# One fused attention, expert and Fourier kernel: value products moved next to the scores, correction products in 128 rows, a relu moved ahead of the folds

## The chip, the cores and the metric

The kernel runs on one core of a Trainium2 chip. The metric is the device time of one execution in microseconds, from the profiler's clock on the chip. Three runs of the kernel before gave 562.93, 563.63 and 563.84 us (median 563.63). TensorE multiplies into PSUM, VectorE and ScalarE read PSUM and work on SBUF, POOL (GpSimd) works on SBUF and issues the indirect transfers, and SP issues most of the other transfers. Each engine runs its own list of instructions in order and waits on semaphores for the others.

## The reference

Three stages in float32. `B,H,S,D` is 2, 8, 768, 64, and the width after the heads are joined is 512.

```python
# attention: a window of 16 around each position, and 24 block maxima of k
k_sum = k.reshape(B, H, nb, block, D).max(axis=3); v_sum = v.reshape(B, H, nb, block, D).mean(axis=3)
scores_l = scale * q @ k.T                      # masked to abs(i-j) < window
scores_s = scale * q @ k_sum.T + np.log(block)
a = softmax(concat([scores_l, scores_s]))       # divided by its sum + 1e-9
x = a @ concat([v, v_sum])
# experts: one of 8 for each token, in order of position
e = argmax(logits) if s == 0 or local_gate < 0.5 else the expert of the token before
out[b, s] = p[e] * (np.maximum(x[b, s] @ w1[e], 0.0) @ w2[e])
# Fourier mix and dense layer
u = x + np.real(fft(fft(x, axis=1), axis=2))
un = (u - mean(u)) / np.sqrt(var(u) + 1e-06)
return u + np.maximum(un @ w_ch1, 0.0) @ w_ch2
```

## The kernel before, in words

**Attention** (`attention`, lines 45 to 257) runs 24 steps t of 128 queries and four heads: 2 batches, 2 groups of heads (a unit u is a batch with a group), 6 chunks. A step is spread over six steps of the loop. `S1(t)` makes the scores on TensorE: two products of the mask `maskb` (69 rows) and sixteen passes of small products of 64 rows and 64 columns (L124), into `sc`. `D1(t)` takes their maximum on VectorE, `A1(t)` the exponentials `a` on ScalarE. Two steps later `S3` transposes `a` into `pa` (L144), `A3` copies it to `att` on ScalarE. One step later again `S4` multiplies `att` with the window of v, `vw`, into `po` (L153): eight products, each into 64 of the 128 partitions, the output's last column being the sum of the weights. `D4` divides on VectorE. `S5` transposes the result into `px` (L169), `A5` copies it to `xT`, and `S6` multiplies it with the gate (L178, into the bank `big`): the logits. So step t on TensorE holds S1 of t, S6 of t-5, S3 of t-2, S4 of t-3 and S5 of t-4, in the order in which the code of the loop calls them. `pa`, `po` and `px` have one buffer each. In steps 8, 13 and 18 `prep_v2` transposes the block means of v (`pv`, L106); ScalarE scales them into `vss` (L108) and copies them into `vw` (L111), ahead of that step's copy of `att`.

**Routing** is a Python generator (`Routing.early`) whose instructions the attention loop takes a few at a time from step 16 on: `ex.d()` gives VectorE's next one, `ex.p()` TensorE's next one, if it is that engine's turn. The logits' first half is copied to `lg` on ScalarE at step 16 (L277). The chain goes by way of the products of `val` (L305, step 17), `lr` (L308, step 18), `cnb` (L329, step 19) and `rinc` (L321, step 20). At L336 it writes the number of the first expert to `ei`; SP reads that and loads the expert's weights (`wr`, 4 of 1 MB, L502). Later it writes the first tokens' indices; POOL gathers them (`xg`, L475). TensorE transposes them (`pt`, L482), and the first expert's products follow (L527).

**Experts** (`moe`): seven slots of 256 tokens, four steps each (L520, L554). The last slot is number 6. `act` applies the relu to `ph` on ScalarE (`hh`, L544) and leaves the residue on VectorE (`hl`, L545); both are operands of `L2` (L554). `out` scales (`y`, L559) and scatters by POOL (L561).

**Fourier mix** (`fft_ffn`, a generator too, whose pieces `next(fft)` puts among slot 6's last products). Sums, differences and halves of rows (`foldE`, `foldP`, `foldO`, `foldQ`, L771 to L787) prepare the operands on VectorE with copies on ScalarE; then products with the tables (L796), corrections of few rows (L811 with 33, L827 with 34 rows), splits into two parts for precision (L767). Batch 0 goes first; `xload(1)` (L722) loads batch 1 once slot 6 is scattered. Then the normalised rows go through the dense layer (L907, L918), where TensorE works without a pause to the end.

The order on each engine is that of the code: nothing moves it afterwards (`manual_schedule`).

Of the kernel before, what the change touches and what calls it, by code (L numbers as in the profile page):

```python
# [15 lines left out]
def keep_warm(nc,I,ps,n):  # L16

    for _ in range(n): nc.tensor.matmul(ps,lhsT=I['busy'][:,0:128],rhs=I['busy'][:,0:ps.shape[-1]],start=True,stop=True)
# [30 lines left out]
def attention(tc,ctx,cp,I,ident,x_dram,plg,late,hook,ex):  # L49
# [3 lines left out]
    with tc.tile_pool(name="at2",bufs=2) as p2, tc.tile_pool(name="at1",bufs=1) as p1, \  # L53
# [94 lines left out]
        def S4(t):  # L148
            u,c=divmod(t,6)
            po=ppo_.tile([128,4,65],F32,name=f"po{t}",tag="po")  # L150
            for g in range(4):
                for jj in range(2):
                    T.matmul(po[64*jj:64*jj+64,g],lhsT=att[t%2][0:121,g,64*jj:64*jj+64],rhs=vw[u][0:121,2*c+jj,g],start=True,stop=True)  # L153
            st['po',t]=po
        def D4(t):
            u,c=divmod(t,6); b,hg=U[u]
# [33 lines left out]
        def at_(f,t):  # L190
            if 0<=t<NT: f(t)
        for t in range(NT+5):
            u,c=divmod(t,6)
            for w in LOADS.get(t,()): load(*w)
            if t<NT:
                at_(S1,t); at_(S6,t-5)
                if t>16: ex.p()
                at_(S3,t-2)
                if t in (8,13,18): prep_v2(u if t<17 else 3)
                if t==3: keep_warm(nc,I,I['idle'],N_B)  # L200
                at_(S4,t-3)
            else: at_(S3,t-2); at_(S4,t-3); at_(S5,t-4); at_(S6,t-5)
            todo=PREP.get(t,())
            at_(D1,t)
            if t<NT:
                if t==16: hook(-1,None)
                if t>16: ex.p()
                at_(S5,t-4)
            at_(D4,t-3)
            for w in todo:  # L210
                if w[0]=='k': prep_k(*w[1:])
            at_(A3,t-2)
            if t==2: keep_warm(nc,I,I['idle'],N_E); prep_v2(0)
            if t==23: at_(A1,t); at_(A5,t-4)
            else: at_(A5,t-4); at_(A1,t)
            for w in todo:
                if w[0]=='k2': prep_k2(*w[1:])
                if w[0]=='v': prep_v(w[1])
            if t==0: load(1,'k'); load(1,'q')
            if t==1: late(); keep_warm(nc,I,WP,N_D); prep_v(0)  # L220
            if t==2: prep_v3(0,V.tensor_copy,2,6); [prep_v3(0,G.tensor_copy,j,j+2) for j in (6,8,10)]
            if t in (8,13,18):
                for j in range(2,12,2): prep_v3(u if t<17 else 3,G.tensor_copy,j,j+2)
            hook(t,psc_)
            if t==NT+4: sctx.close()
# [239 lines left out]
def moe(tc,ctx,fctx,I,ident,idx,sidx,pslot,ei,x_dram,x2_dram,rt,begin,w0,NST=7):  # L465
# [46 lines left out]
    def L1(s,c,fbs=(0,1)):  # L512
        _,wh,wl=Wt[s,c]; xh,xl=X[s][-2:]
        if 0 in fbs: H[s,c]=D['ph'][c%2] if s=='d' else P['ph'].tile([128,2,256],F32,name=f"ph{s}_{c}",tag="ph")
        for fb in fbs:
            n=0
            for kd in range(4):
                o=slice(kd*256+fb*128,kd*256+fb*128+128)
                for a,b in ((wh,xh),(wh,xl),(wl,xh)):
                    T.matmul(H[s,c][:,fb],lhsT=a[:,o],rhs=b[:,kd],start=n==0,stop=n==11); n+=1  # L520
# [20 lines left out]
    def act(s,c):  # L541
        ph=H[s,c]
        hh,hl=D['h'] if s=='d' else [P['p2'].tile([128,2,256],R,name=f"h{n}{s}_{c}",tag=f"h{n}",bufs=2) for n in "hl"]
        S.activation(hh,ph,AF.Relu)  # L544
        V.scalar_tensor_tensor(out=hl,in0=ph,scalar=0.0,in1=hh.bitcast(F32),op0=ALU.max,op1=ALU.subtract)  # L545
        H[s,c]=(hh,hl)
# [33 lines left out]
    for k in range(4,n-1):  # L580
# [4 lines left out]
        s,c=steps[k]  # L585
# [35 lines left out]
            fft=I['fft'](P,D['wr']+[new('up',[128,2048],F32,"wr2","wr",bufs=3)])  # L621

    s=NST-1
    next(fft); L1(s,3); next(fft); act(s,3); L2(s,2,(0,)); next(fft); L2(s,3,(0,)); out(s,tts=(0,)); next(fft); L2(s,2,(1,)); L2(s,3,(1,))
    out(s,tts=(1,)); pctx.close()
    for _ in fft: pass

# [7 lines left out]
def lay_fft():  # L635
    j=np.arange(384)[:,None]; k=np.concatenate([[384,0],np.arange(384)])[None]
    cN=np.cos(2*np.pi*((j*k)%768)/768); cN[:,1]=0
    sN=np.sin(2*np.pi*((j*np.arange(384)[None])%768)/768)
    m=np.arange(256)[:,None]; l=np.arange(258)[None]
    cD=np.cos(2*np.pi*((m*l)%512)/512); cD[:,257]=0  # L640
    sD=np.sin(2*np.pi*((m*np.arange(256)[None])%512)/512)
    out=[]
    for t,n in ((cN,3),(sN,3),(cD,2),(sD,2)):
        for a in _split(t):
            out.append(a.reshape(n,128,-1).transpose(1,0,2).reshape(128,-1))
    ft=np.ascontiguousarray(np.concatenate(out,1)).astype(np.float32)
    corr=np.where(k%2==0,0.0,-2.0); corr[0,1]=0
    alt=np.where(l%2==0,1.0,-1.0)
    rows=np.zeros((34,386+258),np.float32); rows[[0,32],:386]=corr; rows[[0,1,32,33],386:]=alt/2
    return ft,rows  # L650
FT,FROWS=lay_fft()
def lay_ffn(w1,w2):
# [40 lines left out]
class Tables:  # L693

    def __init__(self,tc,I,tp):
        nc=tc.nc
        self.ft=tp.tile([128,FT.shape[1]],R,name="ft"); self.fr=tp.tile([34,644],R,name="fr")
        self.nc=nc; self.I=I
    def load(self,i,n):

# [3 lines left out]
    def parts(self):  # L704
        off=0; tabs=[]
        for w,n in ((386,3),(386,3),(384,3),(384,3),(258,2),(258,2),(256,2),(256,2)):
            tabs.append(self.ft[:,off:off+w*n].rearrange("p (a k) -> p a k",a=n)); off+=w*n
        return tabs,self.fr[0:33,0:386],self.fr[:,386:644]

def fft_ffn(tc,ctx,fctx,tctx,cctx,plctx,I,ident,x2_dram,out,W,P,raw):  # L710

# [43 lines left out]
    if 1:  # L755
# [4 lines left out]
        xo=[unA.tile([128,512],F32,name=f"xo{i}",tag="un",bufs=4) for i in range(4)]; tmp=[xx[:,1542:1800],xo[3][:,0:258]]  # L760
        V.memset(xe[:,:,512:514],0.0)
        V.memset(eps,1e-6); S.activation(nb[:,0:1],eps,AF.Sqrt)
        rP=p1.tile([33,258],R,name="rP"); S.activation(rP,I['busy'][0:33,0:258],AF.Copy,scale=0.0)
        xr=p1.tile([1,512],F32,name="xr")
        S2={}; ST={}; nx=[0]
        def split(dst,src,eng=None):
# [30 lines left out]
        def step1_begin(b):  # L797
            pt,qt=[P['p2'].tile([128,2048],R,name=f"t{n}{b}",tag="w"+n,bufs=3) for n in "hl"]
            ST[b]=([[pt[:,772*mb+386*i:772*mb+386*i+386] for i in range(2)] for mb in range(2)],
                   [[qt[:,768*mb+384*i:768*mb+384*i+384] for i in range(2)] for mb in range(2)],  # L800
                   P['p2'].tile([128,2,256],R,name=f"FF{b}",tag="hh",bufs=2).rearrange("p a b -> p (a b)")[0:34,0:386])
            S.activation(ST[b][2],I['busy'][0:34,0:386],AF.Copy,scale=0.0)
        SP={}
        def step1P(b,a):
            if a==0: SP[b]=[ps1.tile([128,386],F32,name=f"s1_{b}_{mb}",tag="s1") for mb in range(3)]
# [51 lines left out]
            S.copy(U(b,0,1)[0:1],S2.pop(('r',b)))  # L857
            if b==0: S.copy(acc[0:1,:,1],rs[:,0:2])
        yield
        foldE(0,0,V); foldP(0,0); foldO(0,0)  # L860
        yield
        foldE(0,1,V); foldPl(0,0); foldR(0); foldP(0,1)
        yield
# [89 lines left out]
def whole(tc,I,out):  # L953
    nc=tc.nc
    with ExitStack() as ctx:
        ctx.enter_context(tc.manual_schedule())
        cp=ctx.enter_context(tc.tile_pool(name="cp",bufs=1))
        dp=ctx.enter_context(tc.tile_pool(name="dp",bufs=1,space=bass.MemoryType.DRAM))
        x_dram=dp.tile([1664,512],F32,name="x_dram"); x2_dram=dp.tile([1664,512],F32,name="x2_dram")
        ident=cp.tile([128,128],F32,name="ident"); make_identity(nc,ident)  # L960
        busy=cp.tile([128,512],BF,name="busy"); nc.gpsimd.memset(busy,1.0); I=dict(I,busy=busy)
        idx=cp.tile([128,NT2],I32,name="idx"); sidx=cp.tile([128,NT2],I32,name="sidx"); pslot=cp.tile([128,NT2],F32,name="pslot"); ei=cp.tile([1,16],I32,name="ei")
        w0=ctx.enter_context(tc.tile_pool(name="w0",bufs=1)); W={}
        rctx=ExitStack(); rc=rctx.enter_context(tc.tile_pool(name="rc",bufs=1,side="right"))
# [45 lines left out]
```

## Time and profile before

| | us |
|---|---|
| median of three runs | 563.63 |
| the profiled execution's own time | 563.72 |
| its span, first to last instruction | 561.9 |
| TensorE busy | 550.2 (98%) |
| VectorE busy | 313.0 (56%) |
| ScalarE busy | 251.3 (45%) |
| POOL busy | 103.4 (18%) |
| granted clock of TensorE, mean | 1.000 of 2.4 GHz |

A busy share says little here. Matmuls overlap, and their ends are modelled, so TensorE counts as busy while it waits for its array. What a stage is worth is read from starts: when a product begins and when the next one does. The timeline gives for every group the start, the time from its first start to its last end, the engine, the line, what is written and from what, and in brackets how long the engine was idle before it and what ended that. PEld is TensorE's loading of weights, which runs beside its products.

### The profile page before, as it was taken

To read this page: it belongs to the slowest core of one execution; us is meant where nothing else is said; L and a number is where in the kernel's file an instruction comes from. 1 tells how busy PE (TensorE), PEld (TensorE's weight loads), DVE (VectorE), ACT (ScalarE), POOL (GpSimd) and SP (SyncE) were. 2 spreads that over 40 slices of the span, in tenths; PEclk is the share of its full clock that TensorE was granted. 3 is DMA by queue.
4 is the path that set the end of the run, shared out by engine and by line. 5 is a ranking of instruction groups with operands and counts; after the bars stand their busy time and mean duration, and the time that the engine had idled before them with its cause. 6 is when DMAs were issued, how large, how long until landed. Compare 5 with 4: busy or idle time off the path is not lost.

```text
span 561.9 us, 9168 instructions
## 1 busy us (share of the span) xinstructions
PE 550.2 (98%) x3563; PEld 452.0 (80%) x3563; DVE 313.0 (56%) x623; ACT 251.3 (45%) x483; POOL 103.4 (18%) x159
## 2 busy tenths in 40 slices
PE   7999999999999999999999999999999999999997
PEld 3777776799998999978878888888888888888885
DVE  4767837587969786857999798623111103010112
ACT  4777662365767677744454476521221101011010
POOL 3786420300544553411000000000000000000000
PEclk9999999999999999999999999999999999999999
DMA  8997291758988998444033265002000002000001
GB/s 303 408 347 248 87 365 40 264 221 290 362 307 322 366 304 316 139 133 150 2 112 113 89 213 192 34 0 76 0 1 0 1 0 76 0 1 0 1 0 75
DMA packets 21846, 83.70 MB, mean 149 GB/s; under 512 B 2753, under 2 KB 2950, under 8 KB 18216
## 3 DMA queue, kind: packets, MB, share of 16 engines
q1 hardware_dynamic: 18344, 72.23, 35.7%
q0 software_dynamic: 3456, 10.85, 5.5%
q8 instruction: 29, 0.48, 0.3%
q14 instruction: 17, 0.14, 0.1%
HBM read 72.85 MB, written 10.22 MB: 148 GB/s over the span
## 4 chain that ended last, share of the span: by engine, by line
PE 53%; DVE 2%; DMA 0%; issue 0%; ACT 0%; SPq 0%; ACTq 0%
PE fph L907 24%; PE fpy L918 23%; PE s L796 1%; PE s1q L796 1%; PE pp L796 1%; PE py L554 1%; PE pq L796 1%; PE lpt L752 1%; DVE dwr L922 0%; DMA dwr<-x_dram 0%; DVE unl L754 0%; PE s L810 0%; PE s L811 0%; PE pp L827 0%; DVE ch L845 0%
## 5 line engine op out<-in xcount | busy, mean ns | idle before, releaser
L910 DVE SCALAR_TENSOR_TENSOR fhl<-fph,fhh 128x512 fp32r<-128x512 f32 x48 | 33.2, 691 | 150.1 <-ACT fhh L909 150.1
L909 ACT ACTIVATE fhh<-fph 128x512 fp32r<-128x512 f32 x48 | 28.7, 598 | 172.0 <-PE fph L907 172.0
L907 PE MATMUL fph<-unh,fwh 128*128 128x512 f32 x192 | 76.3, 397 | 0.4 <-DVE unl L754 0.4
L907 PE MATMUL fph<-unh,fwl 128*128 128x512 f32 x192 | 75.6, 394 | 0.0
L907 PE MATMUL fph<-unl,fwh 128*128 128x512 f32 x192 | 75.6, 394 | 0.0
L918 PE MATMUL fpy<-fwh,fhh 128*128 128x512 f32 x192 | 75.4, 393 | 0.0
L918 PE MATMUL fpy<-fwh,fhl 128*128 128x512 f32 x192 | 75.3, 392 | 0.0
L918 PE MATMUL fpy<-fwl,fhh 128*128 128x512 f32 x192 | 75.2, 392 | 0.0
L520 PE MATMUL ph<-xx,wh 128*128 128x256 f32 x384 | 68.9, 282 | 0.1
L511 DVE TENSOR_TENSOR wl<-wr,wh 128x1024 fp32r<-128x1024 f32 x50 | 60.0, 1242 | 15.5 <-ACT wh L510 15.5
L520 PEld LDWEIGHTS ph<-xx,wh 128*128 128x128 f32 x384 | 59.6, 188 | 2.0 <-issue 0.5
L510 ACT CAST wh<-wr 128x1024 fp32r<-128x1024 f32 x50 | 49.9, 1049 | 9.9 <-PE py L554 8.6
L520 PE MATMUL ph<-xx,wl 128*128 128x256 f32 x192 | 53.8, 280 | 0.0
L907 PEld LDWEIGHTS fph<-unh,fwh 128*128 128x128 f32 x192 | 36.1, 188 | 8.5 <-DVE unl L754 0.6
L907 PEld LDWEIGHTS fph<-unh,fwl 128*128 128x128 f32 x192 | 36.1, 188 | 8.5
L907 PEld LDWEIGHTS fph<-unl,fwh 128*128 128x128 f32 x192 | 36.1, 188 | 8.0
L918 PEld LDWEIGHTS fpy<-fwh,fhh 128*128 128x128 f32 x192 | 36.1, 188 | 8.0
L918 PEld LDWEIGHTS fpy<-fwl,fhh 128*128 128x128 f32 x192 | 36.1, 188 | 7.9
L918 PEld LDWEIGHTS fpy<-fwh,fhl 128*128 128x128 f32 x192 | 36.1, 188 | 7.9
L554 PE MATMUL py<-wh,hh 128*128 128x512 f32 x100 | 39.8, 398 | 0.9 <-ACT hh L544 0.9
L554 PE MATMUL py<-wh,hl 128*128 128x512 f32 x100 | 39.2, 392 | 0.0
L554 PE MATMUL py<-wl,hh 128*128 128x512 f32 x100 | 39.0, 390 | 0.0
(303 smaller groups left out, 925.9 us busy)
## 6 DMA issues: line engine op xcount, KB each, us to landing
wr<-in_wm SPq DMA_DIRECT2D x28, 1024.0 KB, 6.4
fr<-in_wc SPq DMA_DIRECT2D x32, 512.0 KB, 3.9
vw<-in_vw SPq DMA_DIRECT2D x8, 780.0 KB, 6.1
vT<-in_vT SPq DMA_DIRECT2D x4, 768.0 KB, 6.7
x_dram<-xt SPq DMA_DIRECT2D x12, 256.0 KB, 5.9
dwr<-x_dram SPq DMA_DIRECT2D x12, 256.0 KB, 4.0
out<-dwr SPq DMA_DIRECT2D x12, 256.0 KB, 2.1
ft<-in_ft POOLq DMA_DIRECT2D x7, 417.5 KB, 8.8
```

What stands on the lines that cost most here:

```text
L510: S.copy(wh[:,o],raw[:,o])
L511: eng[i%2].tensor_tensor(out=wl[:,o],in0=raw[:,o],in1=wh[:,o].bitcast(F32),op=ALU.subtract)
L520: T.matmul(H[s,c][:,fb],lhsT=a[:,o],rhs=b[:,kd],start=n==0,stop=n==11); n+=1
L554: T.matmul(PY[s][tt],lhsT=a[:,fb,q],rhs=b[:,o],start=(c==0 and fb==0 and i==0),stop=(c==3 and fb==1 and i==2))
L752: for kd in range(4): T.transpose(pt[:,kd],un[:,kd*128:kd*128+128],ident)
L796: T.matmul(ps,lhsT=ls[l],rhs=rs[r],start=first and n==0,stop=last and n==2); n+=1
L907: T.matmul(ph,lhsT=a[:,kd,o],rhs=x[:,kd],start=n==0,stop=n==11); n+=1
L909: S.activation(hh,ph,AF.Relu)
L910: V.scalar_tensor_tensor(out=hl,in0=ph,scalar=0.0,in1=hh.bitcast(F32),op0=ALU.max,op1=ALU.subtract)
L918: T.matmul(PY[c][t],lhsT=a[:,q],rhs=b[:,k],start=f==0 and i==0,stop=f==15 and i==2)
```

## The change

Four edits. In the attention loop the value products S4 are called right behind the scores, S3 behind them and the logits S6 last (step 3 keeps its order), and S4 reads all 128 rows of `att` and `vw` instead of 121. The corrections' operands (`rP`, `FF`, and the table `fr`) become 128 rows high, zero where there was nothing. Slot 6's last `act` is called ahead of the generator's next piece, and that piece's `foldO` runs on VectorE instead of POOL. The memset of `busy`, the operand of products that only keep TensorE working, moves from POOL to VectorE.

```diff
-                    T.matmul(po[64*jj:64*jj+64,g],lhsT=att[t%2][0:121,g,64*jj:64*jj+64],rhs=vw[u][0:121,2*c+jj,g],start=True,stop=True)
+                    T.matmul(po[64*jj:64*jj+64,g],lhsT=att[t%2][:,g,64*jj:64*jj+64],rhs=vw[u][:,2*c+jj,g],start=True,stop=True)
...
             if t<NT:
-                at_(S1,t); at_(S6,t-5)
+                at_(S1,t)
+                if t==3: at_(S3,1); keep_warm(nc,I,I['idle'],N_B)
+                at_(S4,t-3)
+                if t!=3: at_(S3,t-2)
+                at_(S6,t-5)
                 if t>16: ex.p()
-                at_(S3,t-2)
                 if t in (8,13,18): prep_v2(u if t<17 else 3)
-                if t==3: keep_warm(nc,I,I['idle'],N_B)
-                at_(S4,t-3)
             else: at_(S3,t-2); at_(S4,t-3); at_(S5,t-4); at_(S6,t-5)
...
-    next(fft); L1(s,3); next(fft); act(s,3); L2(s,2,(0,)); next(fft); L2(s,3,(0,)); out(s,tts=(0,)); next(fft); L2(s,2,(1,)); L2(s,3,(1,))
+    next(fft); L1(s,3); act(s,3); next(fft); L2(s,2,(0,)); next(fft); L2(s,3,(0,)); out(s,tts=(0,)); next(fft); L2(s,2,(1,)); L2(s,3,(1,))
...
-    rows=np.zeros((34,386+258),np.float32); rows[[0,32],:386]=corr; rows[[0,1,32,33],386:]=alt/2
+    rows=np.zeros((128,386+258),np.float32); rows[[0,32],:386]=corr; rows[[0,1,32,33],386:]=alt/2
...
-        self.ft=tp.tile([128,FT.shape[1]],R,name="ft"); self.fr=tp.tile([34,644],R,name="fr")
+        self.ft=tp.tile([128,FT.shape[1]],R,name="ft"); self.fr=tp.tile([128,644],R,name="fr")
...
-        return tabs,self.fr[0:33,0:386],self.fr[:,386:644]
+        return tabs,self.fr[:,0:386],self.fr[:,386:644]
...
-        rP=p1.tile([33,258],R,name="rP"); S.activation(rP,I['busy'][0:33,0:258],AF.Copy,scale=0.0)
+        rP=p1.tile([128,258],R,name="rP"); S.activation(rP,I['busy'][:,0:258],AF.Copy,scale=0.0)
...
-                   P['p2'].tile([128,2,256],R,name=f"FF{b}",tag="hh",bufs=2).rearrange("p a b -> p (a b)")[0:34,0:386])
-            S.activation(ST[b][2],I['busy'][0:34,0:386],AF.Copy,scale=0.0)
+                   P['p2'].tile([128,2,256],R,name=f"FF{b}",tag="hh",bufs=2).rearrange("p a b -> p (a b)")[:,0:386])
+            S.activation(ST[b][2],I['busy'][:,0:386],AF.Copy,scale=0.0)
...
-        foldE(0,0,V); foldP(0,0); foldO(0,0)
+        foldE(0,0,V); foldP(0,0); foldO(0,0,V)
...
+        busy=cp.tile([128,512],BF,name="busy"); nc.vector.memset(busy,1.0); I=dict(I,busy=busy)
         ident=cp.tile([128,128],F32,name="ident"); make_identity(nc,ident)
-        busy=cp.tile([128,512],BF,name="busy"); nc.gpsimd.memset(busy,1.0); I=dict(I,busy=busy)
```

TensorE in step 18 of the attention loop, one of the three steps with `pv`, before the change (`sc` scores, `big` logits and routing, `lr` an operand of the routing):

```order
L124 MATMUL sc_1126<-kw_684,qt_744 64x120 x8
L178 MATMUL big<-wgl,xT_1119 128x10 x2
L308 LDWEIGHTS lr_1115
L308 MATMUL big<-identb,lr_1115 128x6
L309 LDWEIGHTS lr_1115
L309 MATMUL big<-identb,lr_1115 128x6
L144 MATMUL pa_1141<-ident,a_1055 120x128 x4
L106 MATMUL pv_1146<-ident,vs_143 120x128 x2
L153 MATMUL po_1151<-vw_566,att_142 64x65 x8
L169 MATMUL px_1169<-ident,xt_2_1110 128x128 x2
```

TensorE in the same step after the change (lines behind 195 are one higher):

```order
L124 MATMUL sc_1126<-kw_684,qt_744 64x120 x8
L153 MATMUL po_1137<-vw_566,att_142 64x65 x8
L144 MATMUL pa_1146<-ident,a_1055 120x128 x4
L178 MATMUL big<-wgl,xT_1119 128x10 x2
L309 LDWEIGHTS lr_1115
L309 MATMUL big<-identb,lr_1115 128x6
L310 LDWEIGHTS lr_1115
L310 MATMUL big<-identb,lr_1115 128x6
L106 MATMUL pv_1155<-ident,vs_143 120x128 x2
L169 MATMUL px_1169<-ident,xt_2_1110 128x128 x2
```

The value products moved from behind the transposes to behind the scores; the logits, the routing's products of `lr` and the transposes `pv` moved behind both.

VectorE between slot 6 and the Fourier mix, before the change (`hl_3` is the residue of slot 6's last part, `xe` and `xo` are the folds' buffers, `dwr` the loaded rows):

```order
L545 SCALAR_TENSOR_TENSOR hl_2_3626<-ph_2_3358,hh_2_3625 128x512
L761 MEMSET xe 128x3x2
L762 MEMSET eps 128x1
L771 TENSOR_TENSOR xe<-dwr_3395 128x512
L774 TENSOR_TENSOR xo_3651<-xe 128x257
L545 SCALAR_TENSOR_TENSOR hl_3_3692<-ph_3_3662,hh_3_3691 128x512
L771 TENSOR_TENSOR xe<-dwr_3395 128x512
L779 TENSOR_TENSOR Pd<-xo_3651,Pd 128x257
```

VectorE at the same place after the change:

```order
L546 SCALAR_TENSOR_TENSOR hl_2_3626<-ph_2_3358,hh_2_3625 128x512
L762 MEMSET xe 128x3x2
L763 MEMSET eps 128x1
L546 SCALAR_TENSOR_TENSOR hl_3_3688<-ph_3_3662,hh_3_3687 128x512
L772 TENSOR_TENSOR xe<-dwr_3395 128x512
L775 TENSOR_TENSOR xo_3651<-xe 128x257
L781 TENSOR_TENSOR xo_3648<-dwr_3395 128x512
L772 TENSOR_TENSOR xe<-dwr_3395 128x512
L780 TENSOR_TENSOR Pd<-xo_3651,Pd 128x257
```

The residue moved ahead of the first fold and its sum, and the subtraction into `xo_3648` came from POOL.

## Rows read from the trace of the kernel before

**Rows 1.** Busy time of each engine (with the number of instructions) in the stretch from 84 to 246 us, then granted clock, DMA share and GB/s.

```profile
84.00:246.00 162.00, 161.78 (x1031) 141.15 (x1032) 123.72 (x201) 102.70 (x149) 52.53 (x46) 1.00 0.74 261
```

**Rows 2.** Timeline of TensorE's products in step 12 of attention up to the scores of step 13, and two groups behind the last scores.

```profile
39.80 0.64 PE L124 MATMUL sc<-kw,qt 64*64 64x120 f32 x16
40.38 0.61 PE L178 MATMUL big<-wgl,xT 128*128 128x10 f32 x4
40.84 0.63 PE L144 MATMUL pa<-ident,a 128*120 128x128 f32 x4
41.40 0.69 PE L153 MATMUL po<-vw,att 121*64 121x65 f32 x16
42.02 0.44 PE L169 MATMUL px<-ident,xt 128*128 128x128 f32 x2
...
42.59 0.64 PE L124 MATMUL sc<-kw,qt 64*64 64x120 f32 x16
...
76.85 0.51 PE L178 MATMUL big<-wgl,xT 128*128 128x10 f32 x4
77.22 0.63 PE L144 MATMUL pa<-ident,a 128*120 128x128 f32 x4
```

**Rows 3.** Timeline of the weight loads, ahead of the value products of step 12 and ahead of the last correction of 33 rows, with the idle time before them.

```profile
41.40 0.55 PEld L153 LDWEIGHTS po<-vw,att 121*64 121x64 f32 x16 [0.17 <-issue]
...
259.22 0.08 PEld L811 LDWEIGHTS s<-fr,rP 33*2 33x2 f32 x1 [0.36 <-issue]
```

**Rows 4.** TensorE's waits: line, what for, us in total, times, the longest.

```profile
PE pt L482 <- DMA xg<-x_dram,idx: 0.7, 1, 0.7
...
PE sc L124 <- DMA qt<-in_qh: 0.4, 1, 0.4
```

**Rows 5.** Timeline of the scores of steps 8, 10, 15 and 18 on TensorE, and of ScalarE's copies in steps 8 and 13.

```profile
27.71 0.64 PE L124 MATMUL sc<-kw,qt 64*64 64x120 f32 x16
...
34.23 0.64 PE L124 MATMUL sc<-kw,qt 64*64 64x120 f32 x16
...
48.75 0.44 PE L124 MATMUL sc<-kw,qt 64*64 64x120 f32 x8
...
57.91 0.64 PE L124 MATMUL sc<-kw,qt 64*64 64x120 f32 x16
...
30.45 0.62 ACT L111 COPY vw<-vss 25x520 f32<-25x520 f32 x1 [0.38 <-POOL kw L94]
31.09 0.59 ACT L147 COPY att<-pa 120x512 f32<-120x512 f32 x1
...
45.62 0.58 ACT L147 COPY att<-pa 120x512 f32<-120x512 f32 x1
```

**Rows 6.** Timeline of the routing in steps 16 to 19: ScalarE's copy of the logits, VectorE's first use of it, the products of lr and cnb on TensorE, VectorE's first use of the latter, and the expert's number.

```profile
52.76 0.22 ACT L277 COPY rlg<-big 128x60 f32<-128x60 f32 x1
...
53.97 0.18 DVE L297 TENSOR_TENSOR rlg<-rlg,big 128x60 f32<-128x60 f32 x1
...
59.03 0.17 PE L308 MATMUL big<-identb,lr 6*128 6x6 bf16 x1
...
62.55 0.17 PE L329 MATMUL big<-cnb,onesb 128*128 128x8 bf16 x1
...
62.76 0.17 DVE L330 SCALAR_TENSOR_TENSOR ky<-big,cst 128x8 f32<-128x8 f32 x1
...
64.53 0.13 DVE L336 CAST ei<-re 1x1 int32<-1x1 f32 x1
```

**Rows 7.** The transfers issued between 64 and 84 us, us from issue to landing (median), for the two gathers of the first tokens; and the same for all gathers of the execution.

```profile
xg<-x_dram,idx POOLq DMA_INDIRECT x2, 7.0
...
DMA to landing us min/median/max: 3.6/7.0/10.3
```

**Rows 8.** Three links of the chain of waits in the Fourier mix: start, us from it to the next link, what.

```profile
256.85 0.53 PE s L796 x3
257.38 0.37 PE s L811
257.75 0.72 PE s L796 x3
```

**Rows 9.** VectorE's waits from 259 to 289 us.

```profile
DVE tl L767 <- ACT tl L767: 1.4, 2, 1.0
...
DVE ch L845 <- ACT cl L843: 0.4, 1, 0.4
```

**Rows 10.** Timeline of TensorE's last products ahead of slot 6's last relu, its residue on VectorE, the second fold of batch 0 and the second fold of batch 1.

```profile
246.78 0.28 PE L520 MATMUL ph<-xx,wl 128*128 128x256 f32 x1
...
249.35 0.69 DVE L545 SCALAR_TENSOR_TENSOR hl<-ph,hh 128x512 fp32r<-128x512 f32 x1 [0.97 <-ACT hh L544]
...
249.96 0.68 DVE L771 TENSOR_TENSOR xe<-dwr 128x512 f32<-128x512 f32 x1
...
265.71 0.69 DVE L771 TENSOR_TENSOR xe<-dwr 128x512 f32<-128x512 f32 x1
```

**Rows 11.** SP's issue of batch 1's six loads (timeline), and us to landing for the first and for the fourth of them.

```profile
259.31 2.69 SPq L722 DMA_DIRECT2D dwr<-x_dram  x6
...
dwr<-x_dram SPq DMA_DIRECT2D x1, 256.0 KB, 2.8
...
dwr<-x_dram SPq DMA_DIRECT2D x1, 256.0 KB, 4.8
```

## The prediction

> **What bounds the kernel now.** I read the busy times by stretch first, then the steady attention step on TensorE, then the waits, and last the stretches that the change touches. From 84 to 246 us TensorE is busy for 161.78 of 162 us [rows 1]: whatever moves the start of that stretch moves its end by as much. Behind 289 us TensorE works alone. So the change is worth what it does to two moments: when the first expert's products begin (84 us) and when the dense layer begins (289 us).
>
> In the attention loop TensorE works through its step in order: scores, logits, transposes, value products, transposes, mask; 42.59 - 39.80 = 2.79 us a step [rows 2]. At the loop's end it waits 0.7 us for the gathered tokens [rows 4]. These took 7.0 us to land where the quickest of all gathers took 3.6 [rows 7]; what they queue behind is 4 MB of the first expert's weights, which SP issues as soon as the expert's number (ei) is written, at 64.53 us [rows 6]. The end of attention hangs on that number, which VectorE's routing makes between the steps' own work; TensorE already waits there.
>
> **Part 1, the value products next to the scores.** Before, each step changes the shape of the array four times: mask to scores, scores to logits, transposes to value products, and back. After it there are three. At such a change the loading of weights stands still, 0.17 us before the value products [rows 3]; and the four logit products take 0.46 us behind the scores (40.38 to 40.84), 0.37 us where no change stands ahead (76.85 to 77.22) [rows 2]. One change costs between 0.09 and 0.20 us. The pair scores and value products is not in the trace; its bounds are nothing and 0.20, and I take a full change, by the nearest row: the product of 33 rows and 2 columns, behind one of 128 rows and 2 columns, has weights idle for 0.36 us [rows 3], so rows alone make a change. The new step is 0.58 scores + 0.62 value products + 0.50 transposes (0.56 less the part of a change behind them) + 0.37 logits + 0.55 (0.57 for transposes and mask, less a part) = 2.62 us, 0.17 less.
>
> By the Trainium skill, TensorEngine Tiling (Array Packing), section Tiling Modes, a change of the tiling mode drains the engine and a change of the tile alone does not. Scores (64 by 64) and value products (128 by 64) are two modes by it, so the pair would pay and the sum stands; were it to pay nothing, the first rival's time would come out. The row with 33 rows agrees; no run here shows the pair itself.
>
> Where does the 0.17 go? I lay the steps out again. In steps 8, 13 and 18 the transposes pv now come 2.07 us after the scores instead of 1.5, and ScalarE, in order, does vss and vw for them before it copies att. Before, the value products used att late in the next step; now they are second in it, and wait.
> - Step 8: its scores at 27.71 - 4 x 0.17 = 27.03. ScalarE's vw waited for POOL until 30.45 and still does, att is done at 31.68; the value products of step 9 start at 31.73, the scores of step 10 at 31.73 + 0.62 + 0.50 + 0.37 + 0.55 = 33.77, 0.46 early [rows 5].
> - Step 13: 0.97 early, pv only 0.41; att is done at 46.20 - 0.41 = 45.79, the scores of step 15 come at 45.84 + 2.04 = 47.88, 0.87 early [rows 5], those of step 16 1.04 early.
> - Step 16: the logits, now fourth, end at the old time (1.04 early, 1.12 later in the step, 0.09 quicker), so ScalarE's copy of them stays at 52.76. But VectorE no longer waits for the value products before it uses it, and starts the routing at 53.0 instead of 53.97 [rows 6]. Step 18 inherits the 0.95.
> - Step 18: the product of lr stands behind the logits, 57.91 - 0.95 + 2.07 + 0.09 = 59.12 [rows 5]; before 59.03 [rows 6].
> - Step 19: att is done 0.39 early at 61.37 (61.76 by the pattern of step 13); then value products, transposes, logits, and the product of cnb at 61.42 + 0.62 + 0.50 + 0.37 = 62.91, before 62.55 [rows 6]. VectorE waits for it where it ran on at 62.76.
>
> So ei comes 0.36 us late, say **+0.4 us**, and with it the weights, the gather and the first expert. Queued behind VectorE's wait stand the rest of the routing and the factors for ScalarE's exponentials. Bounds: -0.6 by the first rival, +1.4 if the steps before gained nothing. That att and vw are read in 128 rows instead of 121 I cost at nothing, as the columns that pass stay the same; bounds 0 and -0.4, the part of a faster step that the waits of steps 9, 14 and 19 would leave.
>
> **Part 2, correction products in 128 rows.** On the chain of waits three products of 128 rows take 0.53 us, the one of 33 rows behind them 0.37, and the three behind that, up to the next of 33 rows, 0.72 [rows 8]. At 0.18 each the four would take 0.71 instead of 1.09, so a 33-row product costs up to 0.38 us beyond itself (the part ahead of the next one is in that); six of them and eight of 34 rows make some 14 x 0.35 = 4.9 us of TensorE between 257 and 288 us. Nearly all is covered by VectorE, whose waits for TensorE by way of ScalarE from 259 to 289 us are tl, 1.4 us, and ch, 0.4 us [rows 9]. The 1.4 us would let it reach the fold at 265.71 [rows 10] some 1.3 us early; but that fold reads the fourth of six loads whose issue begins at 259.31 and takes 2.69 us, so the fourth is issued at 260.65 and, at 4.8 us, lands at 265.4 [rows 11]. The loads follow the scatter of slot 6's second half, which this part doesn't move. Of the 1.3 us some 0.2 is left, and of the wait for ch 0.2, as VectorE gets there earlier itself: **-0.4 us**, bounds 0 and -1.7. The wider table (330 instead of 88 KB on POOL's queue) lies beside TensorE's unbroken work and, at that stretch's 261 GB/s [rows 1], is 0.9 us of transfer if the cover fails.
>
> **Part 3, relu ahead of the folds.** TensorE's last products for slot 6's relu begin at 246.78 and take 0.28 [rows 10]; hh (0.6) no longer stands behind a fold's copy on ScalarE, so hl moves from 249.35 [rows 10] to some 247.7, and TensorE loses a wait like the 0.97 us that VectorE shows there. But all that follows needs the folds, which now start behind hl, with one more operation, the subtraction that POOL did. Hl 0.61 (249.35 to 249.96), the fold 0.68, its sum some 0.4 (half as wide, an estimate from the fold's row) and the subtraction 0.68 (as wide as the fold) take 2.4 us from 247.7: the second fold starts at 250.1, before 249.96 [rows 10]. The scatter and its loads stay in order behind these folds on ScalarE. What TensorE gains it waits for folds: 0, bounds -0.3 and +0.2 (the 0.1 above with the scatter behind it).
>
> **Part 4, the memset of busy on VectorE.** The warming products start earlier, but the second scores still wait 0.4 us for qt's load [rows 4]: 0, bounds -0.4 and +0.2 (VectorE's memset ahead of its first reduction).
>
> Sum against the profiled execution's 563.72 us: +0.4 - 0.4, **563.7 us**. The median of the runs shown is 563.63; the two stand 0.02% apart.
>
> **Rivals.**
> - No change of shape between scores and value products. A step takes 2.45 us; step 9 is still held by POOL's 30.45, but step 18 starts 1.75 early and ei comes 0.6 early: 563.72 - 0.6 - 0.4 = 562.7. For it: both use 64 columns. Against it: the 33-row product.
> - The loads come in time. The fourth took 4.8 us where the first took 2.8 [rows 11]; if that was chance, 1.3 us come through: 563.72 + 0.4 - 1.3 = 562.8. With the first rival it is 561.8.
> - Slower, by the routing. The place is the product of cnb in step 19, behind value products that wait for att. If the change from scores to value products costs as much as the two that it replaces, steps 4 to 16 gain nothing, ei comes 1.4 late and, part 2 at 0, it is 563.72 + 1.4 = 565.1. It decides from an ei about 1.2 us late on. For it: VectorE and the 4 MB are one chain with no cover. Against it: the idle weights that go.
> - The 33 rows are not what costs, but the end of an accumulation: part 2 gives nothing, 563.72 + 0.4 = 564.1.
>
> **Chances.** Forecast 0.45 (its own range 563.0 to 564.5); no change of shape 0.14; loads in time 0.15; both 0.07; slower 0.12; rows don't cost 0.07. Within 0.2% (1.1 us) is about what a measurement can tell from no change. Faster by more: "both" and half of the cases at 562.7 and 562.8, 0.22. Slower by more: most of the slower case and what the forecast and the last rival miss on that side, 0.16. The same 0.62. The range of 562.0 to 564.9 leaves out "both" and most of the slower case.
>
> **What would show it.** A step of 2.6 us with weights idle before scores, value products and the transposes behind them; waits for att in steps 9, 14 and 19; ei near 64.9; correction products 0.18 us apart without idle weights; the fold of 265.71 near its old time, shifted as a whole, waiting for its load. I am wrong if ei comes early, if that fold comes a microsecond early beside the start of its stretch, or if TensorE doesn't wait in step 9.

## The result and the profile after

The changed kernel takes 567.91 us (median of 20 executions, 562.06 to 570.26), the kernel before 563.55 (20 executions, 562.25 to 564.98). The ratio is 1.006, 95% interval 1.0034 to 1.0087: slower, and outside the forecast range.

The 20 times are not one group. In 14 executions the mean granted clock of TensorE is 0.984 to 0.990 and the time 567.3 to 570.3 us; in six it is 0.998 to 1.000 and the time 562.1 to 563.3 (median 562.6). The profiled execution is one of the 14: its own time is 569.45 us, its span 567.6, its clock 0.985. Where the clock holds the change takes some 1 us less than the kernel before, and where it falls some 6 us more than where it holds (median of the 14: 568.6).

| us | before | after |
|---|---|---|
| mask of step 5 | 19.04 | 18.75 |
| mask of step 23 | 72.58 | 71.43 |
| expert's number `ei` | 64.53 | 64.08 |
| first product of the first expert | 83.96 | 87.68 |
| slot 6's last product ahead of its relu | 246.78 | 253.31 |
| first product of the dense layer | 288.75 | 294.46 |

Attention's loop is faster, as meant. The time is lost between 72 and 94 us. The busy times by stretch of the kernel after, TensorE alone (start:end, length, busy with the number of products, granted clock, DMA share, GB/s):

```profile
72.00:74.00 2.00, 2.00 (x42) 1.00 1.06 438
74.00:76.00 2.00, 0.47 (x5) 1.00 0.97 389
76.00:78.00 2.00, 2.00 (x25) 0.66 0.98 312
78.00:80.00 2.00, 2.00 (x19) 0.50 1.00 377
...
90.00:92.00 2.00, 2.00 (x6) 0.50 0.00 0
92.00:94.00 2.00, 2.00 (x6) 0.57 0.00 0
94.00:96.00 2.00, 2.00 (x11) 1.00 0.00 0
```

TensorE does almost nothing from 74 to 76 us, and behind that its clock falls from 2.4 to 1.2 GHz. From the two mixed stretches (0.66 and 0.57) the fall begins at 76.64 and ends at 93.72: 17.1 us at half. "Busy" stays at 2.00 all the while; only the count of products and the clock's column show it. In the kernel before the clock is 1.00 from 72 to 94 us too (stretch, columns as above):

```profile
72.00:94.00 22.00, 20.80 (x195) 1.00 0.53 200
```

What TensorE waited for is in the timeline of the kernel after (start, us, engine, line, operation, and the idle time before it; `DVE` is VectorE, `ACT` ScalarE):

```profile
71.73 0.64 PE L124 MATMUL sc<-kw,qt 64*64 64x120 f32 x16
72.07 1.22 POOL L476 DMA_INDIRECT xg<-x_dram,idx  x1 [1.36 <-DVE idx L275]
72.30 0.69 PE L153 MATMUL po<-vw,att 128*64 128x65 f32 x16
72.92 0.65 PE L144 MATMUL pa<-ident,a 128*120 128x128 f32 x4
73.39 0.66 DVE L130 TENSOR_REDUCE mx<-sc 128x4 f32<-128x480 f32 x1 [1.29 <-PE po L153]
73.59 0.96 POOL L476 DMA_INDIRECT xg<-x_dram,idx  x1 [0.30 <-issue]
73.77 0.42 PE L169 MATMUL px<-ident,xt 128*128 128x128 f32 x2
75.08 0.58 ACT L147 COPY att<-pa 120x512 f32<-120x512 f32 x1 [2.00 <-PE px L169]
75.71 0.65 PE L144 MATMUL pa<-ident,a 128*120 128x128 f32 x4 [1.53 <-ACT att L147]
```

Read it from below. The transposes at 75.71 need `pa`'s one buffer back, so they wait 1.53 us for the copy to `att`. That copy waits for the transposes of 72.92, which by the row end at 73.57, and starts at 75.08. In the same way VectorE's maximum waits for scores that end at 72.37 and starts at 73.39. So the readers of the scores start 1.0 us behind the products' end, those of the transposes 1.5 us, and VectorE's reciprocal, which reads the value products (72.99), starts at 74.96, 2.0 us behind. Each of the three starts comes 0.1 to 0.5 us behind the end of a gather's issue on POOL (73.29 and 74.55). I call these late ends below; the ends of products are modelled by the profile, the readers' starts are not.

The rest of the loop stands as it was laid out. Further rows of the same timeline, with three of TensorE's weight loads:

```profile
38.38 0.37 PE L118 MATMUL sc<-maskb 69*128 69x240 bf16 x2
40.98 0.37 PE L118 MATMUL sc<-maskb 69*128 69x240 bf16 x2
39.25 0.55 PEld L153 LDWEIGHTS po<-vw,att 128*64 128x64 f32 x16 [0.16 <-issue]
39.86 0.41 PEld L144 LDWEIGHTS pa<-ident,a 128*120 128x120 f32 x4
41.27 0.41 PEld L124 LDWEIGHTS sc<-kw,qt 64*64 64x64 f32 x16 [0.20 <-issue]
31.46 0.69 PE L153 MATMUL po<-vw,att 128*64 128x65 f32 x16 [0.39 <-ACT att L147]
62.40 0.17 PE L330 MATMUL big<-cnb,onesb 128*128 128x8 bf16 x1
64.08 0.13 DVE L337 CAST ei<-re 1x1 int32<-1x1 f32 x1
```

A step takes 40.98 - 38.38 = 2.60 us, against 2.79 in [rows 2]. Weights are idle for 0.16 us between scores and value products: that pair does pay for its change of shape. The Trainium skill (TensorEngine Tiling (Array Packing), section Tiling Modes) says that a new mode drains the engine and a new tile alone does not; this row, which the trace before could not show, agrees. The change back behind the value products shows no such pause: the transposes' weights follow 0.06 us behind (39.80 to 39.86).

In the Fourier mix:

```profile
253.31 0.28 PE L521 MATMUL ph<-xx,wl 128*128 128x256 f32 x1
254.32 0.69 DVE L546 SCALAR_TENSOR_TENSOR hl<-ph,hh 128x512 fp32r<-128x512 f32 x1 [3.71 <-ACT hh L545]
254.93 0.68 DVE L772 TENSOR_TENSOR xe<-dwr 128x512 f32<-128x512 f32 x1
262.86 0.34 PE L812 MATMUL s<-fr,rP 128*128 128x386 f32 x1
263.04 0.69 PE L797 MATMUL s<-ft,Pd 128*128 128x386 f32 x3
```

The next products follow a correction 0.18 us behind, where [rows 8] had 0.37. But VectorE now stands still for 3.71 us before `hl`, with the first fold behind it: it waits for `hh`, which ScalarE makes from TensorE's last products.

### The profile page after: what moved, and what is told of

It is laid out like the page before. It is cut to its first block, busy times and chain, and to the rows that moved or that the text cites. A ratio compares the mean times of both kernels' runs of the same rounds, so it can differ in the third digit from the quotient of the medians.

```text
span 567.6 us, 9162 instructions
## 1 busy us (share of the span) xinstructions
PE 551.0 (97%) x3562; PEld 456.9 (80%) x3563; DVE 310.0 (55%) x625; ACT 250.8 (44%) x483; POOL 101.9 (18%) x157
## 3 DMA queue, kind: packets, MB, share of 16 engines
q1 hardware_dynamic: 18344, 72.23, 35.5%
## 4 chain that ended last, share of the span: by engine, by line
PE 48%; DVE 6%; ACT 1%; issue 1%; DVEq 0%; ACTq 0%
PE fph L908 24%; PE fpy L919 23%; DVE xe L772 1%; DVE ch L846 1%; PE lpt L753 1%; DVE xo L781 1%; PE ph L521 1%; DVE dwr L923 0%; DVE unl L755 0%; PE s1q L797 0%; DVE Qd L788 0%; DVE Pd L780 0%; DVE th L768 0%; DVE dwr L855 0%; DVE tl L768 0%
```

## The experiments

Four theories were at stake. A: TensorE's idle time near 74 us is what the clock's fall follows, and the fall is the loss. B: the fall comes from part 4, which starts the warming products earlier. G: the late ends go with the gathers' issue on POOL. And for the mix: part 2 earns, part 3 gives it back.

Three chips were used, and each kernel is compared with the kernel before on the same chip. Chip X: part 1 alone, everything but part 1, the gap filled, part 4 undone. Chip Y: the kernel before again, parts 2 and 3 alone, the old order in the last two steps, and later the changed kernel again with its later gather and the two kernels with unread products ahead of the gathered tokens. Chip Z: the other four. Which chip showed what matters below.

### Parts apart, and the gap filled

**Part 1 alone** (new loop and 128 rows on the kernel before):

> Part 1 alone on the kernel before (new order of attention, 128 rows). Theory A: TensorE's idle 1.5 us near 74 us is what the clock's fall to half follows, and this order makes it: most executions near 568.5 us with a mean clock of 0.985 to 0.99, some near 562.6 with 1.00 (the 1.15 us that attention gained, 72.58 to 71.43 at the last mask). Theory B: the fall comes from the earlier memset and warming products (part 4), which are not in here: all executions near 562.5, clock 1.00.

Measured: median 564.78 us, ratio 1.0018 (0.9986 to 1.0051). Five of 12 executions have clocks of 0.979 to 0.994 (567.3 to 576.2 us), most of the rest 0.999; the kernel before is never under 0.996 on this chip, in 35. The fall is there without part 4, so B falls; it is rarer than expected. In its profiled execution TensorE was idle for 0.7 us at that place, and the clock held.

**Everything but part 1:**

> The changed kernel with part 1 undone (old order, 121 rows), parts 2 to 4 kept. Theory A: clock 1.00 in all executions and 562.8 us, 0.8 less than before (from the last expert product ahead of the folds to the first dense product: 41.15 us in the changed kernel, 41.97 before). Theory B: the fall of the clock stays in most executions, 568 us.

Measured: 563.25 us, ratio 0.9983 (0.9965 to 1.0001), clocks of 0.998 to 1.000 in all 12. The fall belongs to part 1.

**The gap filled.** The changed kernel, plus the line below. It stands in place of one that does nothing here, because its count `N_H` is 0.

```diff
+            if t==23: keep_warm(nc,I,ps.tile([128,512],F32,name=f'warm{t}',tag='sc'),5)
```

> The changed kernel with five products of 512 columns that nobody reads (of the kind that warm TensorE at the start) behind the last scores' step, where TensorE was idle for 1.5 us. Theory A: no fall of the clock, all executions between 562.0 and 562.8 us. Theory B, or a fall that has another cause than the idle time: two groups as in the changed kernel, 562.5 and 568.

Measured: 562.6 us, ratio 0.9972 (0.9952 to 0.9992), no clock below 0.996 in 12. The late ends are still there; only the idle time is gone. Its timeline and its busy times by stretch (columns as above):

```profile
73.79 1.24 PE L18 MATMUL warm<-busy 128*128 128x512 bf16 x5
75.37 0.65 PE L144 MATMUL pa<-ident,a 128*120 128x128 f32 x4 [0.34 <-ACT att L147]
```

```profile
72.00:76.00 4.00, 3.66 (x45) 1.00 1.02 418
76.00:80.00 4.00, 3.87 (x66) 1.00 0.99 342
84.00:88.00 4.00, 4.00 (x20) 1.00 0.01 4
```

Products that nobody reads make the kernel some 5 us faster, by what they keep up: the changed kernel without part 4 takes 567.33 us on the same chip (below). The size fits: from the mask of step 5 to the first expert's first product it is 68.93 us in the kernel after and 64.66 here (18.51 to 83.17), and the products from there to slot 6's last take 165.63 against 163.05: 4.3 + 2.6 = 6.9 of the 7.2 us between the spans (567.6 and 560.4).

**Part 4 undone:**

> The changed kernel with part 4 alone undone: busy's memset on POOL again. Theory A: two groups as in the changed kernel, 562.5 and 568, most executions in the slower one; in the trace TensorE's ends of products near 72 to 75 us come late again. Theory B: all executions near 562.5, clock 1.00.

Measured: 567.33 us, ratio 1.0023 (0.9991 to 1.0056), eight of 12 executions at clocks of 0.985 to 0.990. Late ends again (the last scores' by 1.0 us), idle time 1.4 us. B is refuted from this side too.

**The old order in the last two steps only.** The changed kernel with

```diff
-                at_(S4,t-3)
-                if t!=3: at_(S3,t-2)
+                if t<22: at_(S4,t-3)
+                if t!=3: at_(S3,t-2)
+                if t>=22: at_(S4,t-3)
```

> The changed kernel, but in steps 22 and 23 the transposes go ahead of the value products, as before. Theory A (the idle time near 74 us is what the clock's fall follows; it comes from transposes whose end is told late, behind the value products): the transposes of step 23 end ahead of or between the two gathers, TensorE is idle for under 0.9 us, the clock stays at 1.00, all executions at 562.0 to 563.0 us. Rival (the clock falls because of the new order before step 22): two groups, 562.5 and 568, most in the slower one.

Measured: 562.86 us beside 562.93 for the kernel before, ratio 0.9998 (0.9989 to 1.0007), clocks of 0.998 to 1.000 in all 11. With the transposes ahead of the value products their reader starts between the two gathers (73.48), and the wait that is left near 75 us is

```profile
PE po L153 <- PE pa L144: 0.9, 1, 0.9
```

The changed kernel itself takes 568.05 us on this chip (below). So the loss hangs on two steps of 24. And without the fall the whole change is worth nothing that can be measured here: the 1 us of the first section does not show beside the kernel before on one chip.

### Whose the late ends are

**The kernel before, again:**

> The kernel before, unchanged, in another execution. Theory: the 41.97 us from slot 6's last product to the first dense product hold about 0.9 us of a load that landed late in that one execution (its first fold starts at 246.25 behind the load, in the kernel with part 1 alone at 245.29), so here it is near 41.0; and TensorE's ends of products come late while POOL issues the two gathers near 73 to 76 us, as in the other five traces. Rival: 41.97 again, and no late ends: both belong to the kernel before, and part 1 changed them.

Its one time is 562.12 us. Late ends are here too (the last scores' by 0.3 us, the value products' by 1.0), TensorE is idle for 1.0 us, and the clock is 0.999. The trace on which the forecast rests was one without them. The 41.97 us came out as 41.07; this belongs to the mix, below.

**The gather's issue moved.** The changed kernel with

```diff
+        if s==0: [G.memset(xx,0.0) for _ in range(2)]
```

> The changed kernel with two memsets of 128x2048 on POOL ahead of the first gather's issue (of the gather's own destination, so nothing is computed otherwise), which move that issue from 72.1 to about 74.9 us. Theory G (the ends of TensorE's products are told late while POOL issues the gathers, with the weights' load in flight): none is late near 72 to 74.8 us, those between 74.9 and 77.6 us are. Rival (it is the time and the 4 MB of loads alone, or SP's write of the attention rows): the late ends stay near 72.4 to 75.1 us.

Measured: 566.55 us, ratio 1.0029 (1.0004 to 1.0053), gather at 74.47; no late ends at all, but none either in the other three kernels that ran on chip Z with the gather near 72 us. So it told nothing of G. On chip Y the changed kernel and this one were run side by side:

> The changed kernel once more. If this chip shows late ends of products near 72 to 75 us: idle time of 1.4 to 1.5 us behind them, two groups of times, 562.5 and 568, the slower with a mean clock of 0.985 to 0.987. If it shows none: TensorE waits 0.7 us or more for the gathered tokens near 80 us, and the slower group is at a clock of 0.993 to 0.994 and about 565.5 us.

> The changed kernel with the gather's issue at about 74.5 us again. If the changed kernel shows late ends on this chip: by theory G they are here between 74.5 and 77.3 us and none near 72 to 74 us; by its rival they stay near 72.4 to 75.1 us. If the changed kernel shows none, none here either, and the question stays open.

The changed kernel again: 568.05 us, ratio 1.0061 (1.0025 to 1.0097), late ends (the last scores' by 1.0 us, from 72.23; the value products' by 2.0, from 72.85), idle time 1.5 us, seven of ten at clocks of 0.984 to 0.993:

```profile
73.25 0.66 DVE L130 TENSOR_REDUCE mx<-sc 128x4 f32<-128x480 f32 x1 [1.29 <-PE po L153]
74.83 0.18 DVE L160 RECIPROCAL rs<-po 128x4 f32<-128x4 f32 x1 [0.42 <-PE px L169]
```

The later gather beside it took 566.93 us in its one execution, at a clock of 0.993, with a fall behind a wait of 1.6 us for the gathered tokens. Its timeline:

```profile
72.45 0.69 PE L153 MATMUL po<-vw,att 128*64 128x65 f32 x16 [0.83 <-DVE xt L162]
73.17 0.42 DVE L160 RECIPROCAL rs<-po 128x4 f32<-128x4 f32 x1
73.07 0.65 PE L144 MATMUL pa<-ident,a 128*120 128x128 f32 x4
73.81 0.58 ACT L147 COPY att<-pa 120x512 f32<-120x512 f32 x1 [0.93 <-PE pa L144]
73.87 1.22 POOL L477 DMA_INDIRECT xg<-x_dram,idx  x1 [0.30 <-DVE rs L160]
75.04 0.69 PE L153 MATMUL po<-vw,att 128*64 128x65 f32 x16
75.98 0.18 DVE L160 RECIPROCAL rs<-po 128x4 f32<-128x4 f32 x1 [1.91 <-PE po L153]
```

Value products and transposes of 72.45 and 73.07 are now told within 0.1 us of their end (73.14 and 73.72): their readers start at 73.17 and 73.81. So the late ends near 72 to 74 us are gone when the gather's issue comes later: the first half of G holds. The second half, that they come with the issue, hardly shows. The value products that end at 75.73 release VectorE at 75.98, 0.25 us behind, where the same group on chip Z has 0.04 (76.32 to 76.36); no other reader is later than there. The two memsets also hold up VectorE, and with it the value products (0.83 us), so more than the gather's time differs. That the issue itself causes the late ends is not shown. Why one chip shows none, and why later gathers, which are issued with less load traffic, show none, stays open too.

### The second gap, at the gathered tokens

On chip Z, without late ends, the clock fell in another way, to means of 0.993 to 0.996, and behind another gap: the wait for the gathered tokens, the wait of 0.7 us in [rows 4]. The kernel before was not spared there: 10 of its 29 executions there have clocks of 0.993 to 0.996.

**Old order in 22 and 23, part 3 undone:**

> As the kernel with the old order in steps 22 and 23, and part 3 undone: no unread products. Theory: clock 1.00 in all executions; from slot 6's last product to the first dense product 40.2 (early load) or 41.2 us (late load); 562.4 us, 0.4 under the kernel with the old order in steps 22 and 23 and part 3. Rival (part 3 neutral): no difference to it.

Measured on chip Z: 564.41 us, ratio 1.0016 (0.9997 to 1.0036), nine of 12 at clocks of 0.993 to 0.996. Against the expectation the clock fell, and the trace shows where (timeline, then stretches):

```profile
80.60 0.66 PE L484 MATMUL pt<-ident,xg 128*128 128x128 f32 x4 [1.12 <-DMA xg<-x_dram,idx]
81.59 0.66 PE L484 MATMUL pt<-ident,xg 128*128 128x128 f32 x4 [0.34 <-DMA xg<-x_dram,idx]
```

```profile
80.00:82.00 2.00, 1.06 (x8) 1.00 1.06 407
82.00:84.00 2.00, 2.00 (x13) 0.53 0.36 138
84.00:86.00 2.00, 2.00 (x7) 0.50 0.07 20
```

**The same with five unread products ahead of those transposes:**

```diff
+            if t==26: keep_warm(nc,I,ps.tile([128,512],F32,name='warm26',tag='sc'),5)
```

> The kernel with the old order in steps 22 and 23 and without part 3, with five unread products of 512 columns (1.1 to 1.2 us) ahead of the transposes of the gathered tokens. Theory A (idle time of TensorE there is what the clock's fall follows): clock 1.00 in all or nearly all executions, and a median of 561.8 to 562.3 us. Rival (that wait is not the cause): clocks of 0.994 in most, as in 9 of 12 without these products, 564.4 us.

Measured on chip Y: 562.27 us, ratio 0.9984 (0.9963 to 1.0005), clocks of 0.997 to 1.000 in all 12. This is what theory A expects, but it doesn't test A: on chip Y the kernel with the old order in steps 22 and 23, without these products, kept its clock as well (0.998 to 1.000 in all 11), and the falls that should go away were seen on chip Z. So at the second gap A is argued from the traces, not shown: the falls of the four kernels of chip Z, and of the later gather, start at the end of the waits for the tokens or up to 1.5 us behind them. By the Trainium skill (TensorE: Matmul & The Clock Gate, section HAM oscillation — how this bites in real kernels) products that are broken by waits for transfers make the engine fall back to the slow clock, and the next burst starts in it. The trace at the second gap agrees (clock 0.53 in the stretch behind waits of 1.12 and 0.34 us). The waits in the page's example are longer than these, though, and at the first gap the wait is for ScalarE's copy and not for a transfer; the measurement decides.

### The Fourier mix

**Part 2 alone**, **part 3 alone**, and two without part 3:

> Part 2 alone on the kernel before. Prediction: products with the tables and corrections 0.18 us apart, and from the first product of the mix to the first dense product 34.89 - 0.4 = 34.5 us. Rival (VectorE's own work sets that stretch, and no wait of it is for TensorE): 34.9 again.

> Part 3 alone on the kernel before. Prediction: from slot 6's last product to the first dense product the same as before (41.97 with the late load, 41.03 without it) within 0.3 us: what TensorE gains ahead of the mix (7.1 or 6.1 us becomes 5.6) it gives back inside it. Rival (the gain comes through): 40.5 us.

> The changed kernel with the five unread products in the gap, and part 3 undone (relu and foldO where they were). Theory (part 2 earns 0.8 to 0.9 us and part 3 gives 0.4 of it back): from slot 6's last product to the first dense product 40.2 us where the first fold's load comes early, 41.2 where it comes late; clock 1.00; 562.0 us, about 1 us under the kernel before. Rival (part 3 neutral): 41.1 us, and the time of the kernel with the five products and part 3.

> The changed kernel without part 3, with five unread products in the first gap and three ahead of the gathered tokens. Theory A: clock 1.00 in nearly all, a median of 561.5 us, at least 1.5 us under the kernel before. Rival (the unread products delay what they stand ahead of by as much as they save): 562.5 us.

Part 2 alone took 562.52 us in its one execution, and 33.95 us from the mix's first product to the dense layer where 34.5 was expected. Part 3 alone took 563.45 us in its one execution, and its 41.46 us below are 0.4 more than the early value that it was expected to keep.

From slot 6's last product ahead of its relu to the first dense product, and the part of it up to the mix's first product, both by the timelines:

| kernel | load of the first fold | to the mix, us | to the dense layer, us |
|---|---|---|---|
| before | late | 7.08 | 41.97 |
| before, again | early | 6.18 | 41.07 |
| part 1 alone | early | 6.14 | 41.03 |
| part 2 alone | late | 7.21 | 41.16 |
| parts 1, 2, 4, first gap filled | early | 6.07 | 40.07 |
| parts 1, 2, 4, both gaps filled | late | 6.98 | 40.97 |
| part 3 alone | (hidden) | 5.59 | 41.46 |
| all four | (hidden) | 5.63 | 41.15 |

The first fold, `xe`, needs two loads. In the three late traces the second one lands 3.8 to 4.0 us behind its issue; in the early trace with the first gap filled it takes 2.9. With a late load the fold starts about 0.9 us later. In the kernel before, again, and with part 3 alone, VectorE's first fold stands so (timelines):

```profile
244.83 0.69 DVE L771 TENSOR_TENSOR xe<-dwr 128x512 f32<-128x512 f32 x1 [1.27 <-DMA dwr<-x_dram]
247.92 0.69 DVE L545 SCALAR_TENSOR_TENSOR hl<-ph,hh 128x512 fp32r<-128x512 f32 x1 [0.97 <-ACT hh L544]
248.53 0.68 DVE L771 TENSOR_TENSOR xe<-dwr 128x512 f32<-128x512 f32 x1
```

```profile
248.05 0.69 DVE L545 SCALAR_TENSOR_TENSOR hl<-ph,hh 128x512 fp32r<-128x512 f32 x1 [3.71 <-ACT hh L544]
248.66 0.68 DVE L771 TENSOR_TENSOR xe<-dwr 128x512 f32<-128x512 f32 x1
```

Part 2 earns 0.8 us with a late load (41.97 to 41.16) and 1.0 with an early one (41.07 to 40.07; 40.06 and 40.16 in the two kernels with the old order in steps 22 and 23). VectorE's waits for TensorE show it: for `tl` 0.8 us instead of 1.4, for `ch` 0.2 instead of 0.4, as in [rows 9]. Part 3 costs 0.4 us alone (41.07 to 41.46) and 1.1 beside part 2 (40.07 to 41.15) when the load is early, since VectorE waits 3.7 us in order for `hh` while the fold behind could run. Only against a late load, and without part 2, does it help (41.97 to 41.46). The all-four row is 41.15: the two cancel when the load is early.

Times of the combinations: first gap filled, without part 3, 561.66 us, ratio 0.9958 (0.9937 to 0.9978), on chip Z, where the kernel before has falls; both gaps filled (three unread products at the second), without part 3, 562.19 us, ratio 0.9982 (0.9965 to 0.9998), on chip Y. The second was expected 1.5 us under the kernel before and is 1.0. Both beat the kernel before, and the second the changed kernel on its chip (568.05); no chip ran the two side by side, so which is better is not told.

**121 rows again:**

> The changed kernel with the value products in 121 rows again, order as changed. Prediction: the step stays at 2.60 us between the masks of steps 10 to 13. Rival (121 rows are one more change of shape, to the transposes of 128 rows): 2.7 to 2.8 us, as before the change.

The steps take 2.60 us (masks of steps 11 and 12 at 35.76 and 38.36): the rows do not matter. Its one time, 565.29 us at a clock of 0.993, is one with a fall at the second gap.

## Why the prediction was wrong

- **What failed: TensorE's waiting was priced at nothing beyond its length.** The working followed the loop up to `ei` in step 19 and stopped there, with "TensorE already waits there". Steps 22 to 25 were not laid out. There part 1 puts the transposes behind the value products, so that their end falls into the gathers' issue, and TensorE idles for 1.5 us. The sum has no term for a clock: the fall costs about 6 us, more than any bound in the prediction.
- **The trace before hid half of it.** It showed no late ends; its other execution did. With part 1 the idle time that they make is longer in three traces (1.4 to 1.5 us, against 0.9 to 1.0 in the old order), but not in that of part 1 alone (0.7, where the clock held).
- **The step: right.** 2.60 us measured, 2.62 forecast; weights idle before scores and before value products, but not before the transposes behind them; the wait for `att` in step 9 as laid out. The rival in which the pair pays nothing is refuted, and 128 rows are free.
- **`ei`: wrong in sign, small.** Forecast 0.36 us late; counted from the mask of step 5 it is 45.33 us instead of 45.49, and 45.57 with part 1 alone. The product of `cnb`, counted the same way, comes at 43.65 instead of 43.51: 0.14 us late, not 0.36. The rival that was slower by the routing is refuted: slower came by another way.
- **That attention's end hangs on `ei`, the 4 MB and the gather: right.** The loop from step 5 to 23 is 0.86 us shorter (52.68 for 53.54), but the first expert starts 65.21 us behind step 5 with the old order in two steps, 65.03 and 64.92 in the two traces before. The saved time becomes waiting at the second gap, and that is not free either.
- **Part 2: mechanism right, size off.** 0.8 to 1.0 us measured, 0.4 forecast. The working held it back by the fourth load; VectorE shows no wait at that fold in any trace without part 3, and with part 3 in two (0.3 and 0.4 us). The rival "the loads come in time" is nearer. That rows don't cost is refuted.
- **Part 3: the term was mis-sized.** 0 forecast with a bound of +0.2; +0.4 alone and +1.1 beside part 2. Its working was right by itself: the second fold starts 3.28 us behind slot 6's last product, by the forecast 3.3. But it was compared with a trace whose first fold had a late load (3.18 there), and with an early load that fold starts 2.27 us behind.
- **Part 4: nothing, as forecast.** Two groups of times with it and without it.

With the clock held, 562.86 us beside 562.93 is the "no change" of the forecast, but by luck: of its two terms the +0.4 for `ei` did not come, the -0.4 for part 2 was -0.8 to -1.0, and part 3 gave about as much back. The time was lost where the sum had no term.

## What to carry to other kernels

A wait of TensorE costs more than its length when the clock falls behind it: read the column of the granted clock by stretch, in several executions, before a wait is called free. A reordering that saves TensorE time ahead of a fixed transfer turns that time into waiting; if the gap can't be closed by other work, a few products that nobody reads may be worth more than they cost. And one profiled execution has chance in it (a late load, late ends): a term that rests on one start time wants a second trace.

## What the runs showed beyond that

TensorE's ends reached VectorE and ScalarE up to 2.0 us late while POOL issued the first gathers beside 4 MB of loads: in all twelve experiments on chips X and Y (with the later gather only by 0.25 us), in none of the four on chip Z. Idle length alone does not decide the clock: 1.4 to 1.5 us near 74 us was followed by a fall in all three traces that have it, 0.7 to 1.0 us there in none, and near 80 us two waits of 0.3 us for the tokens were followed by one in the trace with the first gap filled and without part 3, where the kernel before kept its clock behind 0.7 us [rows 4]:

```profile
PE pt L483 <- DMA xg<-x_dram,idx: 0.7, 2, 0.3
```

What else decides stays open. And while POOL wrote the two memsets of the later gather (3.67 us from 69.91), a reciprocal of 128x4 on VectorE took 1.95 us instead of 0.18:

```profile
69.78 1.95 DVE L160 RECIPROCAL rs<-po 128x4 f32<-128x4 f32 x1
69.91 3.67 POOL L474 MEMSET xg<- 128x2048 f32 x2
```
